# Router logits on four column tiles, fewer count products, scatters without order between them, and a few background steps at other places

## The chip, the cores and the metric

One Trainium2 chip, and the kernel runs on one of its cores. The metric is the device time of one execution in microseconds (us), of which the median over runs counts. TensorE is called PE (its weight loads PEld), VectorE DVE, ScalarE ACT, GpSimd POOL, and SyncE, which issues most DMA transfers, SP.

## The reference

Three layers follow one another. B = 2, S = 768, H = 8 heads of 64, D = 512.

1. Attention: each query row sees the first 8 columns and the last 96 before it, with a linear bias by distance (a slope for each head), softmax, and a product with v.
2. A mixture of 8 experts (512 to 1024 to 512). Each row has eight logits `x @ w_gate` and a local gate `x @ w_local`. The row's own best expert is taken if the local gate is under 0.5, else the expert of the row before it (so the choice is a scan along the sequence). Only the chosen expert is computed, and its output is scaled by the softmax of the logits at that expert.
3. A channel mix: each row is mixed with the row before it, `k = relu(xk @ w_k)`, `out = sigmoid(xr @ w_r) * (k*k @ w_v)`. The last weights come as 64-bit floats and are decoded by integer operations.

All products are to be as good as float32. A float32 product is one matmul in the code and two records of PE in the trace. Expert products are made of three single-pass products, of the upper and lower parts of both operands (`whi`, `wlo` for weights; `xh`, `xl` for rows). A transpose is one record.

## The kernel before

The attention loop (lines 1112 to 1198) has an iteration i for every half of the heads of a tile t of 128 rows: t = i // 2, g = i % 2. The whole program is under a manual schedule: every engine runs its instructions in the order in which the lines emit them. An iteration emits: transposes of the probabilities of i-1 (`emit_pT`, bank PT), the point "Ra", exponentials of i (`emit_exp`, ACT), copies of the transposes out of PSUM (`emit_ev`, the first on DVE, the second on ACT), in odd i the copy of the attention output `emit_xT`, the point "Dm", a step of background work for the first expert (`bg_early`), scores of the next tile (`emit_S`, in odd i), in even i transposes of k and q, in odd i the transposes of a finished tile (`turn_x`), the point "Rb", another `bg_early`, the minima of i+1 (`emit_min`, four DVE passes over the scores, which also add the bias), `route_x` in odd i (DVE scales the turned tile to X), the point "Db", in even i the products with v (`emit_pv`), "Rc", "Dc", and at most one scatter. In the trace, iteration 9 begins at 41.53 us, 13 at 58.32, 17 at 74.99, 18 at 80.60, 19 at 86.42, 20 at 91.17, 21 at 96.43, 22 at 103.14, and the part written out after the loop (lines 1200 to 1282) at 107.92.

The router works on groups of two tiles. `plan` hangs its steps on the named points of iterations (`at`, `do`): logits (`route_lg`, line 200: for every tile four products with xT as the weights, 128 columns, and 18 moving columns of `wgb`), their row maxima (`route_max`, `route_max2`), a transpose to rows (`route_rows`), the scan (`route_scan`, DVE), back to columns (`route_turn`), one-hot (`route_oh`), counts (`route_sum`, lines 273 and 275: `tri[:, 0]` sums the rows before in the tile, `tri[:, 1]` all rows of an earlier tile, `acc` is the sum of earlier groups), and positions (`route_pos`, line 291 on). All of them use one PSUM bank, R. The last group runs behind the loop, between steps of the first expert.

After the third and the fourth group `order_a` and `order_b` (lines 311 to 326) rank the experts by the rows so far, and `early_start` reads the number of the likely first and second expert into SP, which then loads its weights. `bg_early` moves the first expert on by a step: it loads a chunk of weights, makes the lower part of one half chunk on DVE (`w_lo1`, line 630) and the upper part of the next one on ACT (`w_hi1`, line 625), which it appends to `lo_q`. `F_(m)` runs m steps of the first expert's products.

`scatter` (line 283) writes the 128 rows of X of a tile to their places in the DRAM tensor `xs` by an indirect DMA that POOL issues. Behind the scatter of tile 7 SP loads the first rows of the first expert (`early_x`, line 948), behind that of tile 9 the next. From 113 us on PE runs the experts, and from about 300 us the channel mix.

Of the kernel before, what the change touches and what calls it, by code (L numbers as in the profile page):

```python
# [8 lines left out]
F32 = mybir.dt.float32  # L9
# [7 lines left out]
P = 128  # L17
# [27 lines left out]
FREE = 4  # L45
NIN = 4
# [7 lines left out]
class Net:  # L54
# [29 lines left out]
    def routing_consts(self):  # L84
# [4 lines left out]
        self.wgb = c.tile([P, KD, 2, E + 1], F32, name="wgb")  # L89
# [47 lines left out]
    def gate_rest(self):  # L137
        for a in range(2):
            r = slice(a * HD, (a + 1) * HD)
            self.nc.gpsimd.tensor_copy(self.wgb[r, :, a, :], self.wg[r, :, :])  # L140
# [53 lines left out]
    def route_lg(self, g, t, xT, tag="R"):  # L194
        nc = self.nc
        if t == g[0]:
            self.lgp = self.bank(tag, 2 if tag == "PT" else 1)
        for kk in range(KD):
            o = ((t - g[0]) * H + 2 * kk) * (E + 1)
            nc.tensor.matmul(self.lgp[:, o:o + 2 * (E + 1)], lhsT=xT[:, kk, :],  # L200
                             rhs=self.wgb[:, kk, :, :].rearrange("p a c -> p (a c)"), start=True, stop=True)

    def route_max(self, pool, g):
        nc, n, t0 = self.nc, len(g), g[0]
        lh = pool.tile([P, n * H, E + 1], F32, tag="lh", bufs=1, name=f"lh{t0}")
        nc.vector.tensor_tensor(lh, self.lgp[:, 0:n * H * (E + 1)].rearrange("p (a c) -> p a c", c=E + 1),
                                self.RI[:, t0:t0 + n, :].rearrange("p a h -> p (a h)").unsqueeze(2).to_broadcast([P, n * H, E + 1]), op=ALU.mult)
# [59 lines left out]
    def route_sum(self, pool, g):  # L267
        nc, n, t0 = self.nc, len(g), g[0]
        pp = self.bank("R", 1)
        for i in range(n):  # L270
            rest = [self.OHr[:, t0 + a, :] for a in range(i)] + ([self.acc] if self.acc is not None else [])
            o = pp[:, i * E:(i + 1) * E]
            nc.tensor.matmul(o, lhsT=self.tri[:, 0, :], rhs=self.OHr[:, t0 + i, :], start=True, stop=not rest)
            for a, x in enumerate(rest):
                nc.tensor.matmul(o, lhsT=self.tri[:, 1, :], rhs=x, start=False, stop=a == len(rest) - 1)
        one = self.tri[:, 1, 0:1].bitcast(F32)
        parts = [self.OHr[:, t, :].bitcast(F32) for t in g] + ([self.acc.bitcast(F32)] if self.acc is not None else [])
        for a, x in enumerate(parts):
# [299 lines left out]
def build(ctx, tc, ins, out):  # L578
# [4 lines left out]
    n.xs = n.dram.tile([E * REG, D], F32, name="xs")  # L583
    ys = n.dram.tile([ROWS, D], F32, name="ys")
# [387 lines left out]
    def lg(g):  # L972
        for t in g:
            n.route_lg(g, t, xTs[t])

# [7 lines left out]
    for g in groups:  # L983
        i = 2 * g[-1] + 3
        lgg, mx, mx2, rows, scan, tn, oh, sm_, ps_, acc = (lambda f=f, g=g: f(ap2, g) for f in (
            lambda _, g: lg(g), n.route_max, n.route_max2, n.route_rows, n.route_scan, n.route_turn, n.route_oh, n.route_sum,
# [4 lines left out]
        at(i, "Rb", lgg)  # L991
        at(i + 1, "Dm", mx, mx2)
# [16 lines left out]
        if g[-1] in (5, 7):  # L1009
            e = g[-1] == 7  # L1010
            at(i + 3, "Db", lambda e=e: n.order_a(ap2, "fg"[e], n.cnte if e else n.cnt6, n.fvec if e else None))
            at(*((i + 4, "Ra") if e else (i + 3, "Dc")), lambda e=e: n.order_b(ap2, "fg"[e], rp))
            at(i + 4, "Rb", lambda e=e: early_start(3 * e, e))

    with tc.manual_schedule():
# [96 lines left out]
        for i in range(NI - 1):  # L1112
# [40 lines left out]
            emit_min(i + 1)  # L1153
# [8 lines left out]
            if scq:  # L1162
                scatter(scq.pop(0))
# [52 lines left out]
        emit_ev(i - 1, 0)  # L1216
        emit_ev(i - 1, 1, True)
# [10 lines left out]
        while hi_q or lo_q:  # L1228
            bg_early()
# [3 lines left out]
        oh()  # L1233
        emit_pT(i, 0)
# [728 lines left out]
```

## Time and profile before

| | |
|---|---|
| device time, median of 3 runs (lowest, highest) | 487.65 us (485.9, 492.04) |
| the profiled execution's own time | 488.38 us |
| its span from the first to the last instruction | 486.3 us |
| PE busy | 469.6 us, 97% of the span |
| DVE, ACT, POOL busy | 344.4, 265.5, 114.4 us |
| mean granted clock of PE | 0.99 of full speed |

Times in the rows are in us from the start of the span. A row of a timeline has its start, its length, the engine, the line, the operation, out<-in and shapes, how many instructions were merged into it, and in brackets how long the engine was idle before it and for whom. The length of a matmul holds the time until its result is there, so lengths overlap, and the distance between two starts is what one costs. A row of a table by stages has the stretch, its length, and for each engine the time that it was busy and its instructions; then PE's granted clock (1.00 is 2.4 GHz, 0.50 is 1.2 GHz), the share of the DMA engines, and GB/s.

### The profile page before, as it was taken

What the parts mean: (1) busy time and instruction counts of PE and PEld (TensorE: products, weight loads), DVE (VectorE), ACT (ScalarE), POOL (GpSimd) and SP (SyncE); (2) the same over time, 40 slices, a digit from 0 to 9 for tenths busy, and PEclk for the clock granted to TensorE, in tenths of its full rate; (3) what the DMA queues carried; (4) which work ended last, traced back from release to release, by engine and by line L of the source; (5) the groups of instructions that cost most, each with busy time, mean ns of one, the idle gap of its engine ahead of it and who ended that gap; (6) DMA issues with size and microseconds to landing.
All of it is one profiled execution on the core that took longest, in us unless ns stands there. A gap on an engine that the chain in (4) does not pass through costs nothing. (4 is left out here: it accounts for less than half of the span.)

```text
span 486.3 us, 9258 instructions
## 1 busy us (share of the span) xinstructions
PE 469.6 (97%) x3211; PEld 407.0 (84%) x3211; DVE 344.4 (71%) x911; ACT 265.5 (55%) x652; POOL 114.4 (24%) x200
## 2 busy tenths in 40 slices
PE   7999999889999999999999999999999999999994
PEld 5788888778788989878978887798989899898984
DVE  7877796696875885897898888797857768264301
ACT  4787876764536554757587776862433414152320
POOL 4111212112110000010010013051754918253220
PEclk9999998989999999999999999999999999999998
DMA  9998585962775978598699753003836442200001
GB/s 181 266 234 165 145 175 153 290 201 83 255 278 167 355 207 325 171 345 288 238 344 378 278 177 97 34 1 90 301 109 246 146 155 82 65 23 23 22 3 49
DMA packets 76492, 86.90 MB, mean 179 GB/s; under 512 B 50677, under 2 KB 50933, under 8 KB 76437
## 3 DMA queue, kind: packets, MB, share of 16 engines
q1 hardware_dynamic: 68176, 63.01, 42.3%
q0 software_dynamic: 4944, 17.17, 10.9%
q10 hardware_dynamic: 3316, 6.03, 3.4%
q8 instruction: 28, 0.46, 0.4%
q14 instruction: 28, 0.22, 0.2%
HBM read 73.49 MB, written 12.71 MB: 177 GB/s over the span
## 5 line engine op out<-in xcount | busy, mean ns | idle before, releaser
L625 ACT ACTIVATE whi<-wraw 128x512 fp32r<-128x512 f32 x128 | 72.5, 623 | 6.1 <-ACTq L717 2.3
L634 DVE TENSOR_TENSOR wlo<-wraw,whi 128x1024 fp32r<-128x1024 f32 x55 | 66.0, 1217 | 2.7 <-ACT whi L625 2.5
L1474 ACT ACTIVATE sq<-S 128x256 f32<-128x256 f32 x48 | 18.5, 385 | 74.4 <-PE S L643 71.3
L641 PE MATMUL S<-xkh,whi 128*128 128x256 f32 x192 | 54.5, 284 | 0.2 <-ACT whi L625 0.2
L643 PE MATMUL S<-xkh,wlo 128*128 128x256 f32 x192 | 53.6, 279 | 0.2 <-DVE wlo L630 0.2
L642 PE MATMUL S<-xkl,whi 128*128 128x256 f32 x192 | 53.5, 279 | 0.0
L1484 POOL TENSOR_TENSOR kl<-sq,kh 128x256 fp32r<-128x256 f32 x40 | 36.5, 921 | 71.1 <-issue 37.4
L1514 DVE TENSOR_TENSOR o<-O,sig 128x512 f32<-128x512 f32 (+1 forms) x13 | 8.4, 649 | 51.9 <-PE O L643 31.7
L642 PE MATMUL O<-wlo,kh 128*128 128x512 f32 (+1 forms) x104 | 39.3, 378 | 0.3 <-DVE wlo L630 0.3
L643 PE MATMUL O<-whi,kl 128*128 128x512 f32 (+1 forms) x104 | 39.3, 378 | 0.0
L641 PE MATMUL O<-whi,kh 128*128 128x512 f32 (+1 forms) x104 | 39.1, 376 | 0.0
L641 PEld LDWEIGHTS S<-xkh,whi 128*128 128x128 f32 x192 | 36.4, 190 | 0.7 <-ACT whi L625 0.4
L643 PEld LDWEIGHTS S<-xkh,wlo 128*128 128x128 f32 x192 | 36.0, 188 | 0.4 <-DVE wlo L630 0.4
L642 PEld LDWEIGHTS S<-xkl,whi 128*128 128x128 f32 x192 | 36.1, 188 | 0.3
L1475 DVE SCALAR_TENSOR_TENSOR sq<-S,sq 128x256 f32<-128x256 f32 x48 | 20.1, 420 | 16.4 <-ACT sq L1474 16.0
L1483 ACT ACTIVATE kh<-sq 128x256 fp32r<-128x256 f32 x48 | 19.7, 412 | 12.0 <-DVE sq L1475 12.0
L892 ACT ACTIVATE zbig<-zbig,nm 128x232 f32<-128x232 f32 (+1 forms) x48 | 22.4, 466 | 5.9 <-DVE nm L880 5.9
L283 POOL DMA_INDIRECT xs<-X,posi x12 | 12.5, 1045 | 53.1 <-DVE acc L301 21.1
L642 PEld LDWEIGHTS O<-wlo,kh 128*128 128x128 f32 x104 | 19.6, 188 | 4.6 <-DVE wlo L630 0.7
L641 PEld LDWEIGHTS O<-whi,kh 128*128 128x128 f32 x104 | 19.6, 188 | 3.8
L643 PEld LDWEIGHTS O<-whi,kl 128*128 128x128 f32 x104 | 19.6, 188 | 3.7
L892 ACT ACTIVATE peb<-peb,nm 128x232 f32<-128x232 f32 (+1 forms) x48 | 22.2, 463 | 0.0
(461 smaller groups left out, 1423.0 us busy)
## 6 DMA issues: line engine op xcount, KB each, us to landing
wraw<-in_moe_w_dram SPq DMA_DIRECT2D x64, 512.0 KB, 5.7
dwt<-in_moe_w_v_dram POOLq DMA_DIRECT2D x8, 512.0 KB, 4.6
z<-in_moe_w_k_dram SPq DMA_DIRECT2D x8, 512.0 KB, 4.2
z<-in_moe_w_v_dram SPq DMA_DIRECT2D x8, 512.0 KB, 4.8
ys<-yo ACTq DMA_DIRECT2D x13, 256.0 KB, 6.5
vn<-in_v_dram SPq DMA_DIRECT2D x12, 256.0 KB, 4.1
xn<-xs SPq DMA_DIRECT2D x12, 256.0 KB, 5.3
dwt<-in_moe_w_k_dram POOLq DMA_DIRECT2D x6, 512.0 KB, 6.8
```

The source lines that it names most:

```text
L283: self.nc.gpsimd.indirect_dma_start(self.xs, bass.IndirectOffsetOnAxis(ap=self.posi[:, t:t + 1], axis=0), X[t], None)
L625: nc.scalar.activation(out=whl[r, c][0][:, sl], in_=raws[r, c][:, sl], func=ACTF.Copy)
L634: nc.vector.tensor_tensor(lo, raws.pop((r, c)), hi.bitcast(F32), op=ALU.subtract)
L641: nc.tensor.matmul(out_, lhsT=ah, rhs=bh, start=first, stop=False)
L642: nc.tensor.matmul(out_, lhsT=ah, rhs=bl, start=False, stop=False)
L643: nc.tensor.matmul(out_, lhsT=al, rhs=bh, start=False, stop=last)
L892: nc.scalar.activation(out=pe, in_=pe, func=ACTF.Exp, scale=-1.0, bias=nm[:, h:h + 1], accum_out=sm[:, h:h + 1])
L1474: nc.scalar.activation(out=sq_, in_=ps[:, 0:TB], func=ACTF.Relu)
L1475: nc.vector.scalar_tensor_tensor(sq_, ps[:, 0:TB], 0.0, sq_, op0=ALU.max, op1=ALU.mult)
L1483: nc.scalar.activation(out=hh, in_=sq_, func=ACTF.Copy)
L1484: (nc.gpsimd if b else nc.vector).tensor_tensor(hl, sq_, hh.bitcast(F32), op=ALU.subtract)
L1514: nc.vector.tensor_tensor(o[:, a:z], ps[:, 0:z - a], sig[b, i][:, a:z], op=ALU.mult)
```

## The change

The logits of the first five groups get another form. `wgb`, now padded to 32 columns for each of the four 128-row chunks, is the weights, and xT moves with 128 columns; the four chunks stand on four column tiles of PE (`route_lgt`, at the place of the old products). ACT copies the result to SBUF (`route_lge`, at "Db"), and one iteration later PE transposes it, once for each tile (`route_lgb`, at "Ra"). The last group keeps the old form with the new padding. `route_sum` makes the positions of a group in three products (two in the first group) in place of five (three). The scatters write through views of `xs` that are declared disjoint, so that none waits for another, and the end of an iteration may issue two of them. `bg_early` leaves the newest entry of `lo_q` for the next call while the loop runs. For the second ranking, `order_a` goes from "Db" of iteration 20 to "Db" of 19, right behind the positions, and `order_b` from "Ra" of 21 to "Ra" of 20. The minima of iteration 23 go from the loop's last iteration to the part behind it, behind a copy out of PSUM.

```diff
-        self.wgb = c.tile([P, KD, 2, E + 1], F32, name="wgb")
+        self.wgb = c.tile([P, KD, GW], F32, name="wgb")
...
+    def route_lgt(self, pool, g, xTs):
+        nc, n = self.nc, len(g)
+        bank = self.bank("R", 1)
+        for i, t in enumerate(g):
+            for kk in range(KD):
+                nc.tensor.matmul(bank[kk * GW:(kk + 1) * GW, i * P:(i + 1) * P], lhsT=self.wgb[:, kk, :], rhs=xTs[t][:, kk, :],
+                                 start=True, stop=True, tile_position=(0, kk * GW))
+        self.lgp = bank
+
+    def route_lge(self, pool, g):
+        n = len(g)
+        self.lgt = pool.tile([P, 2, P], F32, tag="lgt", bufs=1, name=f"lgt{g[0]}")
+        self.nc.scalar.activation(out=self.lgt[:, 0:n, :], in_=self.lgp[:, 0:n * P].rearrange("p (a c) -> p a c", a=n), func=ACTF.Copy)
+
+    def route_lgb(self, pool, g):
+        self.lgp = self.bank("R", 1)
+        for i in range(len(g)):
+            self.nc.tensor.transpose(self.lgp[:, i * P:(i + 1) * P], self.lgt[:, i, :], self.ident)
...
-        for i in range(n):
-            rest = [self.OHr[:, t0 + a, :] for a in range(i)] + ([self.acc] if self.acc is not None else [])
-            o = pp[:, i * E:(i + 1) * E]
-            nc.tensor.matmul(o, lhsT=self.tri[:, 0, :], rhs=self.OHr[:, t0 + i, :], start=True, stop=not rest)
-            for a, x in enumerate(rest):
-                nc.tensor.matmul(o, lhsT=self.tri[:, 1, :], rhs=x, start=False, stop=a == len(rest) - 1)
+        parts = [(0, n, self.tri[:, 0, :], self.OHr[:, t0:t0 + n, :].rearrange("p a e -> p (a e)"))]
+        if self.acc is not None:
+            parts.append((0, n, self.tri[:, 1, :], self.acc.unsqueeze(1).to_broadcast([P, n, E])))
+        if n > 1:
+            parts.append((1, n, self.tri[:, 1, :], self.OHr[:, t0, :]))
+        for i, (a, z, w, x) in enumerate(parts):
+            nc.tensor.matmul(pp[:, a * E:z * E], lhsT=w, rhs=x, start=i == 0, stop=i == len(parts) - 1)
...
-        self.nc.gpsimd.indirect_dma_start(self.xs, bass.IndirectOffsetOnAxis(ap=self.posi[:, t:t + 1], axis=0),
+        self.nc.gpsimd.indirect_dma_start(self.xviews[t], bass.IndirectOffsetOnAxis(ap=self.posi[:, t:t + 1], axis=0),
...
+    n.xviews = dram_disjoint_views(n.xs, NTT)
...
         at(i, "Rb", lgg)
+        at(i, "Db", lambda g=g: n.route_lge(ap2, g))
+        at(i + 1, "Ra", lambda g=g: n.route_lgb(ap2, g))
...
-            at(i + 3, "Db", lambda e=e: n.order_a(ap2, "fg"[e], n.cnte if e else n.cnt6, n.fvec if e else None))
-            at(*((i + 4, "Ra") if e else (i + 3, "Dc")), lambda e=e: n.order_b(ap2, "fg"[e], rp))
+            at(i + 3 - e, "Db", lambda e=e: n.order_a(ap2, "fg"[e], n.cnte if e else n.cnt6, n.fvec if e else None))
+            at(i + 3, "Ra" if e else "Dc", lambda e=e: n.order_b(ap2, "fg"[e], rp))
...
-        def bg_early():
+        def bg_early(keep=1):
             if ld_q:
                 w_load(0, ld_q.pop(0))
-            for u in lo_q[:1]:
+            for u in lo_q[:1] if len(lo_q) > keep else ():
...
-            emit_min(i + 1)
+            if i < NI - 2:
+                emit_min(i + 1)
...
-            if scq:
+            for _ in scq[:2]:
                 scatter(scq.pop(0))
...
         emit_ev(i - 1, 0)
+        emit_min(i)
         emit_ev(i - 1, 1, True)
...
-        while hi_q or lo_q:
-            bg_early()
+        for _ in range(2):
+            bg_early(0)
         emit_pv(i - 1, 0)
         emit_pv(i - 1, 1)
         tn()
         oh()
+        while hi_q or lo_q:
+            bg_early(0)
```

## Rows read from the trace of the kernel before

**Rows 1.** Busy time by stages: one group of the loop, its last iterations, the experts.
```profile
58.32:74.99 16.67, 16.06 (x165) 13.80 (x163) 13.79 (x64) 12.66 (x44) 2.55 (x7) 1.00 0.70 153
91.17:107.92 16.75, 14.17 (x139) 12.07 (x136) 14.86 (x65) 12.10 (x36) 2.54 (x3) 0.90 0.72 219
153.00:300.00 147.00, 145.82 (x853) 126.47 (x852) 121.77 (x205) 97.21 (x197) 11.46 (x20) 1.00 0.77 268
```
**Rows 2.** The same view of the two stretches in which the granted clock fell.
```profile
80.80:84.20 3.40, 3.40 (x18) 3.07 (x18) 2.45 (x15) 1.75 (x6) 0.00 (x0) 0.50 0.99 263
104.50:107.90 3.40, 3.40 (x33) 3.09 (x32) 3.23 (x17) 2.57 (x7) 0.00 (x0) 0.53 0.97 287
```
**Rows 3.** Timeline of PE in iterations 5 and 6: logits, transposes, products with v.
```profile
27.61 1.86 PE L200 MATMUL R<-wgb,xT 128*128 128x18 f32 x16
29.32 0.31 PE L899 MATMUL PT<-ident,zbig 128*128 128x128 f32 x1
...
30.23 0.60 PE L823 MATMUL S<-ident,kn 128*128 128x128 f32 x4
30.66 0.60 PE L823 MATMUL S<-ident,qn 128*128 128x128 f32 x4
31.46 0.39 PE L924 MATMUL O<-pt,vp 128*64 128x128 f32 x4
31.68 0.39 PE L924 MATMUL O<-pt,vn 128*64 128x128 f32 x4
```
**Rows 4.** Timeline of ACT around the logits of iteration 13.
```profile
63.54 0.39 ACT L908 ACTIVATE pt<-PT 128x256 f32<-128x256 f32 x1 [1.95 <-PE PT L899]
```
**Rows 5.** Timeline of PE: first and last of the five count products of a group.
```profile
55.56 0.25 PE L273 MATMUL R<-OH,tri 128*128 128x8 f32 x1
...
56.01 0.25 PE L275 MATMUL R<-acc,tri 128*128 128x8 f32 x1
```
**Rows 6.** Timeline of PE before the first fall of the clock, and during it.
```profile
78.79 1.96 PE L200 MATMUL R<-wgb,xT 128*128 128x18 f32 x16 [0.24 <-DVE fi L339]
...
82.15 1.06 PE L823 MATMUL S<-ident,kn 128*128 128x128 f32 x4
```
**Rows 7.** Timeline of PE: its two longest waits of the loop.
```profile
93.10 0.30 PE L899 MATMUL PT<-ident,zbig 128*128 128x128 f32 x1 [1.28 <-DVE mm L291]
...
98.43 0.20 PE L320 MATMUL R<-dgg,ones 8*8 8x8 f32 x2 [0.91 <-DVE dgg L315]
```
**Rows 8.** Timeline of DVE in iterations 19 to 21.
```profile
90.39 0.69 DVE L630 TENSOR_TENSOR wlo<-wraw,whi 128x512 fp32r<-128x512 f32 x1 [1.96 <-ACT whi L625]
...
92.87 0.16 DVE L291 SCALAR_TENSOR_TENSOR mm<-iota_e,R 128x16 f32<-128x16 f32 x1
...
93.80 0.67 DVE L910 COPY pt<-PT 128x512 f32<-128x512 f32 x1
...
97.98 0.15 DVE L313 SCALAR_TENSOR_TENSOR keyg<-Rf,keyg 8x1 f32<-8x1 f32 x1
98.16 0.22 DVE L315 TENSOR_SCALAR dgg<-ident,keyg 8x8 f32<-8x8 f32 x1
```
**Rows 9.** Timeline of ACT: first split of the first expert, and that of its fifth chunk.
```profile
89.74 0.61 ACT L625 ACTIVATE whi<-wraw 128x512 fp32r<-128x512 f32 x1
...
112.39 1.14 ACT L625 ACTIVATE whi<-wraw 128x512 fp32r<-128x512 f32 x2
```
**Rows 10.** Timeline of POOL: the scatters of tiles 6 and 7.
```profile
93.93 1.00 POOL L283 DMA_INDIRECT xs<-X,posi  x1 [3.69 <-DVE acc L301]
99.46 0.96 POOL L283 DMA_INDIRECT xs<-X,posi  x1 [4.54 <-DMA xs<-X,posi]
```
**Rows 11.** Timeline of SP: the fifth chunk, and the first rows of the first expert.
```profile
90.68 2.10 SPq L596 DMA_DIRECT2D wraw<-in_moe_w_dram  x1
102.28 0.36 SPq L948 DMA_DIRECT2D xe<-xs  x1
```
**Rows 12.** The page's part on DMA issues: size and median us to landing.
```profile
wraw<-in_moe_w_dram SPq DMA_DIRECT2D x64, 512.0 KB, 5.7
```

More of the change, by code (lines that the diff above doesn't have):

```diff
@@ L5 @@
 from concourse import mybir
+from concourse.ap import dram_disjoint_views
 from concourse._compat import with_exitstack
@@ L45 @@
 FREE = 4
+GW = 32
 NIN = 4
@@ L139, in gate_rest @@
             r = slice(a * HD, (a + 1) * HD)
-            self.nc.gpsimd.tensor_copy(self.wgb[r, :, a, :], self.wg[r, :, :])
+            self.nc.gpsimd.tensor_copy(self.wgb[r, :, a * (E + 1):(a + 1) * (E + 1)], self.wg[r, :, :])
     def mix_rest(self):
@@ L198, in route_lg @@
         for kk in range(KD):
-            o = ((t - g[0]) * H + 2 * kk) * (E + 1)
+            o = ((t - g[0]) * KD + kk) * GW
             nc.tensor.matmul(self.lgp[:, o:o + 2 * (E + 1)], lhsT=xT[:, kk, :],
-                             rhs=self.wgb[:, kk, :, :].rearrange("p a c -> p (a c)"), start=True, stop=True)
+                             rhs=self.wgb[:, kk, 0:2 * (E + 1)], start=True, stop=True)
+    def route_lgt(self, pool, g, xTs):
[14 more added lines that the diff above has]
+            self.nc.tensor.transpose(self.lgp[:, i * P:(i + 1) * P], self.lgt[:, i, :], self.ident)
     def route_max(self, pool, g):
@@ L205, in route_max @@
         lh = pool.tile([P, n * H, E + 1], F32, tag="lh", bufs=1, name=f"lh{t0}")
-        nc.vector.tensor_tensor(lh, self.lgp[:, 0:n * H * (E + 1)].rearrange("p (a c) -> p a c", c=E + 1),
-                                self.RI[:, t0:t0 + n, :].rearrange("p a h -> p (a h)").unsqueeze(2).to_broadcast([P, n * H, E + 1]), op=ALU.mult)
+        nc.vector.tensor_tensor(lh.rearrange("p (m a) c -> p m a c", a=2),
+                                self.lgp[:, 0:n * P].rearrange("p (m r) -> p m r", r=GW)[:, :, 0:2 * (E + 1)].rearrange("p m (a c) -> p m a c", a=2),
+                                self.RI[:, t0:t0 + n, :].rearrange("p t (k a) -> p (t k) a", a=2).unsqueeze(3).to_broadcast([P, n * KD, 2, E + 1]), op=ALU.mult)
         lp = self.LS[:, t0:t0 + n, :]
@@ L970, in do @@
             f()
-    def lg(g):
-        for t in g:
-            n.route_lg(g, t, xTs[t])
     def pos(g):
@@ L985, in build @@
         lgg, mx, mx2, rows, scan, tn, oh, sm_, ps_, acc = (lambda f=f, g=g: f(ap2, g) for f in (
-            lambda _, g: lg(g), n.route_max, n.route_max2, n.route_rows, n.route_scan, n.route_turn, n.route_oh, n.route_sum,
+            lambda _, g: n.route_lgt(ap2, g, xTs), n.route_max, n.route_max2, n.route_rows, n.route_scan, n.route_turn, n.route_oh, n.route_sum,
             lambda _, g: pos(g), n.route_acc))
```

## The prediction

> **What bounds the kernel now.** I read the busy time by stages first. In the experts PE is busy for 145.82 of 147 us, and in one group of the router's loop for 16.06 of 16.67 [rows 1]: PE's own work sets the time, and what is saved in the loop should reach the end, since the work behind it is PE's as well. One stretch is different. From 91.17 to 107.92 PE is busy for only 14.17 of 16.75 us and DVE for 14.86: here the two hold each other up. The same view gives the granted clock, which fell to 0.50 and 0.53 in two stretches of 3.4 us, at 80.8 and at 104.5 [rows 2]. Last I read the timelines, since a length of a matmul overlaps the next, and only the distance of starts is a price [rows 3].
>
> **Logits.** Now: two tiles by four products by two records, from 27.61 to 29.32 (the first transpose behind them), 1.71 us, 0.107 a record [rows 3]. After: again 16 records, but on four column tiles, then two transposes. A transpose costs (30.66 - 30.23) / 4 = 0.11 [rows 3], so 0.22. The products with v show two column tiles: four records of 128 moving columns take 31.68 - 31.46 = 0.22, two at a time at 0.11 [rows 3]. Four column tiles are in no row. The low end is four at a time, 16 / 4 x 0.11 = 0.44; the high end one after the other, 16 x 0.11 = 1.76. The nearest row overlaps fully, so I take 0.50, a little over the low end. Passing into the tiled form costs something: the eight transposes from 30.23 are over at 31.09, and the second four of the v products start at 31.46, so the first four had 0.37 in place of 0.22, 0.15 more. Passing back I take as 0.10 (nothing and 0.15 are its ends). Sum 0.22 + 0.50 + 0.25 = 0.97, and 0.74 saved in a group. Four of the five groups lie before iteration 19, where PE sets the time: 2.95 us. The fifth, in iteration 21, lies in the stretch that DVE holds up, and I count it as nothing (0.74 is its end).
>
> **The copy and the waits of this path.** The ACT copy is 128x256, 0.39 us as the copy of that size at 63.54, ahead of which ACT had been idle for 1.95 us [rows 4]; that idle time hides it. ACT waits for PE there, and what queues behind it are exponentials whose minima come later anyway. Without cover it would be 0.39 in each of five groups, 2 us. PE's transposes of the copy stand behind the eight transposes of the probabilities, 8 x 0.11 = 0.9 us of work, against 0.39 and the two hand-overs. Where a batch begins there are only four of those, and a wait of up to 0.4 is the end. The shared bank R is free at both places but one: the logits still wait for the rank's read, as the 0.24 at 78.79 [rows 6]. The larger memset and the regrouped read of DVE move the same 144 columns: nothing.
>
> **Counts.** Five products of 0.11 (55.56 to 56.01 is four) [rows 5] become three: 0.22 saved, 0.11 in the first group. Six groups give 1.21. Those of the fourth and fifth group fall where DVE sets the time; the rest is 0.11 + 3 x 0.22 = 0.77. The doubled width, 16 columns, costs nothing that a row would show.
>
> **The clock.** A stretch of 3.4 us at half clock costs 3.4 x (1 - 0.50) = 1.7, the second 1.6 [rows 2]. Just before the first fall PE stood still for the rank (0.24 and the result's way before it) and then ran the logits, which move 18 columns a record for 1.8 us [rows 6]; the second follows logits of the same kind behind the second ranking's read. The group from 58.32, whose logits have no such wait, ran at 1.00 [rows 1]. After the change the long run of tiny moves becomes a short one of full width, and I expect the first fall to go: 1.7 us. The second lies over DVE's stretch: nothing (1.6 is its end). The Trainium skill (TensorE: Matmul & The Clock Gate, Part 4: PE-mode transpose) says that transposes do not count as busy for the clock, and this speaks against the change, which takes real products out of a run of transposes; by it both falls stay. The trace bears it out in part only: the half clock ended at 84.2 though nearly all that ran in it were transposes, such as the four of 1.06 us at 82.15 [rows 2, 6]. That result is a rival below.
>
> **The lower parts, the keys, the minima.** Now DVE waits 1.96 us at 90.39 for the upper part that ACT begins only at 89.74 [rows 8, 9], and the minima of iteration 20 and X stand behind it; PE then waits 1.28 at 93.10, and 0.91 at 98.43 for the ranking's key [rows 7]. With the newest entry left in the queue the lower part follows an upper part that is a call old, so the 1.96 goes. Late next is the ranking: `order_b` now stands on PE ahead of the transposes of k and q, and waits for the counts' whole chain, 93.80 - 92.87 = 0.93 from first step to the sum of groups and 0.40 for the key (97.98 to 98.38) [rows 8]. Against it PE has the eight transposes of the probabilities, 0.9 us, so PE waits some 0.5 to 0.9 here, in place of the 0.91 later; on DVE the steps of `order_b` stand ahead of the next copy out of PSUM, which waits as long. Then one more lower part, 0.6 us, falls behind the loop, and the minima of 23 (1.3 us) stand between a copy and the scan there; DVE's amount of work is the same. What can be had: at most the 1.96 and DVE's idle 16.75 - 14.86 = 1.89 [rows 1], 3.85; less the new wait, 0.7, and the 0.6 behind the loop, 2.5. I take 2.0. The ends are 0, if the new wait eats it, and 3.85.
>
> **Scatters.** The wait of 4.54 on POOL goes [rows 10]. POOL does nothing else that is urgent, so it is worth nothing by itself; two issues in a row hold POOL for 2.0 us, and the copies of the global columns behind them have as long until their scores are there. But SP's queue is reordered: the read of the first expert's rows, which waits for both scatters, now stands ahead of a v tile, a v window and the fifth weight chunk, which went out at 90.68 while the read went out at 102.28 [rows 11]. With the second scatter issued some 4.5 us earlier the read goes at about 98, the chunk at about 99, and it lands by its median of 5.7 [rows 12] at about 105; ACT first reads it at 112.39, less what the loop gains, about 106 [rows 9]. Covered by an us: nothing; without cover some 3.
>
> **The sum.** 2.95 + 0.77 + 1.7 + 2.0 = 7.4 us. From the profiled execution's own 488.38 that gives 481.0; that execution was 0.73 over the median shown, so against the median 487.65 the sum gives 480.3. 2% is 9.75 us, about what a measurement of this kernel can tell from no change.
>
> **Rivals.**
> - The clock falls as before (the rule above, at work on this kernel's transposes): 480.3 + 1.7 = 482.0; a fall at each of the three other logits too, as products leave them, adds 1.7 each, up to 487. For it: nearly all of the work around the logits is transposes. Against it: the clock's return at 84.2.
> - PE alone sets the time all along, DVE keeping up: 5 x 0.74 + 1.21 + 1.7 + 1.6 + 1.28 + 0.91 = 10.4, so 477.2. Against it: DVE is busy for 89% of the last iterations [rows 1].
> - The column tiles don't overlap: 1.76 for 0.50 in four groups and part of the fifth adds about 5.5: 486. Against it: the v products.
> - Slower: each step from one column tile to the next costs what passing into the tiled form does, 0.15 a record. Then the products take 16 x 0.26 = 4.2 and a group 4.6 in place of 1.71, five groups 14.6 more; with the falls of the clock left, and 0.77 and 2.0 gained, 11.8 slower: 499. It decides from (2.95 + 0.77 + 2.0) / 5, about 1.1 us over my 0.50 for a group's products. Against it: the v products step between two tiles at no price.
>
> **How the numbers follow.** My forecast 0.50, the clock as before 0.20, PE alone 0.16, no overlap 0.08, slower 0.06. The range is 476.5 to 486.0: it takes in the first three but the lowest of the PE case (0.06), and leaves out the slower case, the repeated falls and a part of no overlap (0.12). Faster by over 2%, under 477.9: most of the PE case, 0.12, and the low edge of the forecast, where DVE's gain goes to its end, 0.07: 0.19. Slower by over 2%: 0.05 of the slower case. The rest, 0.76, is within 2%.
>
> **What would show it.** Logits: 16 short records from first to last start in about 0.5 us and a group's loop 0.7 shorter. Counts: three records. Clock: 1.00 throughout the loop. Lower parts: no idle DVE ahead of line 630, and PE's largest wait in iteration 20 at line 320, under 1 us. Scatters: pairs 1 us apart, and the read of the first expert's rows some 4 us earlier. I am wrong if the 16 records take over 1 us, if the clock falls at other places, or if ACT waits for the fifth chunk.

## The result and the profile after

The changed kernel takes 481.62 us (median of six runs, 480.93 to 483.31) against 488.12 us for the kernel before (six runs, 485.9 to 492.04): a ratio of 0.9865, with a 95% interval of 0.9824 to 0.9905. The forecast was 480.3 us in a range of 476.5 to 486.0, and within 2% as the likeliest outcome; it held. In the two profiled executions the span falls from 486.3 to 479.4 us, 6.9 us against the 7.4 of the sum. How that 6.9 is made up is another matter, and most of what follows is about it.

First the page of the kernel after: the engines' busy time and share of the span.

```profile
PE 460.3 (96%) x3210; PEld 395.9 (83%) x3210; DVE 344.9 (72%) x911; ACT 266.4 (56%) x657; POOL 115.1 (24%) x200
```
Busy time by stages, against [rows 1, 2]; the columns are the stretch, its length, then busy time and instructions of PE, PEld, DVE, ACT and POOL, the granted clock, the DMA share and GB/s.

```profile
80.80:84.20 3.40, 3.40 (x46) 2.88 (x44) 2.70 (x19) 2.45 (x10) 0.00 (x0) 1.00 0.86 278
104.50:107.90 3.40, 2.90 (x29) 2.17 (x25) 3.40 (x9) 3.20 (x11) 0.00 (x0) 1.00 0.30 110
87.71:101.70 13.99, 11.62 (x141) 9.51 (x139) 12.01 (x53) 11.69 (x36) 2.55 (x3) 1.00 0.81 239
24.00:106.60 82.60, 76.71 (x856) 64.36 (x853) 66.99 (x300) 66.68 (x217) 13.83 (x29) 1.00 0.72 200
153.00:300.00 147.00, 145.23 (x852) 125.35 (x851) 122.12 (x210) 96.75 (x198) 13.89 (x22) 1.00 0.76 265
```
The clock is at 1.00 (2.4 GHz) in the two stretches where it had fallen to half, and in the whole of 24.00 to 106.60; the experts' stage is as full as before. In the last iterations, 87.71 to 101.70, PE is busy for 11.62 of 13.99 us. Its idle time there is 2.37 us, hardly less than the 2.58 of before: the stretch became shorter by the work in it, and a larger share of it is waiting.

The timeline of PE, in order of time; the columns are start, length, engine, line, operation, tiles and shape, and in brackets the idle time before it and who ended it. Most lines of the loop are 22 to 24 higher in the new kernel; the making of `X` is line 188 (186 before).

```profile
7.61 0.44 PE L863 MATMUL PT<-ident,kn 128*128 128x128 f32 x2
7.89 0.38 PE L863 MATMUL PT<-ident,qn 128*128 128x128 f32 x2
...
27.45 0.64 PE L210 MATMUL R<-xT,wgb 128*32 128x128 f32 x16
28.03 0.33 PE L923 MATMUL PT<-ident,zbig 128*128 128x128 f32 x1
...
28.96 0.38 PE L222 MATMUL R<-ident,lgt 128*128 128x128 f32 x2
...
45.98 0.30 PE L923 MATMUL PT<-ident,zbig 128*128 128x128 f32 x1 [1.01 <-DVE X L188]
...
54.81 0.26 PE L298 MATMUL R<-OH,tri 128*128 128x16 f32 x1
...
55.03 0.25 PE L298 MATMUL R<-OH,tri 128*128 128x8 f32 x1
...
61.66 0.30 PE L923 MATMUL PT<-ident,zbig 128*128 128x128 f32 x1 [0.38 <-DVE X L188]
...
79.21 0.30 PE L923 MATMUL PT<-ident,zbig 128*128 128x128 f32 x1 [0.73 <-DVE X L188]
...
89.61 0.19 PE L343 MATMUL R<-dgg,ones 8*8 8x8 f32 x2 [0.79 <-DVE dgg L338]
...
99.03 0.30 PE L923 MATMUL PT<-ident,zbig 128*128 128x128 f32 x1 [1.34 <-DVE X L188]
...
106.64 0.48 PE L665 MATMUL S<-whi,exexh 128*128 128x512 f32 x1
```
These answer to [rows 3, 5, 6, 7]. The sixteen records of a group's logits now run from 27.45 to 28.03, 0.58 us where they took 1.71; the counts of a group are three records, 0.11 apart. New are the four waits for `X` (line 188): 1.01, 0.38, 0.73 and 1.34, 3.46 us together. Before, PE had one such wait in the loop's later part, of 0.15 us. The bank in which the new transposes of x stand must be read by DVE before PE may fill it again with probabilities, and the long logits used to run in just that time. The first product of the first expert starts at 106.64; in the execution of before it started at 112.73. I use this record as the loop's end below.

The other engines, against [rows 8 to 11]: the scatters on POOL, the reads on SP, the fifth chunk's split on ACT, and one wait on DVE.

```profile
89.03 1.00 POOL L306 DMA_INDIRECT xs<-X,posi  x1 [2.02 <-DVE keyg L334]
90.33 0.97 POOL L306 DMA_INDIRECT xs<-X,posi  x1 [0.31 <-issue]
```
```profile
93.76 0.34 SPq L972 DMA_DIRECT2D xe<-xs  x1
...
94.79 0.43 SPq L620 DMA_DIRECT2D wraw<-in_moe_w_dram  x1
```
```profile
106.08 1.14 ACT L649 ACTIVATE whi<-wraw 128x512 fp32r<-128x512 f32 x2
```
```profile
45.14 0.69 DVE L188 TENSOR_TENSOR X<-PT,RI 128x512 f32<-128x512 f32 x1 [0.97 <-DMA xs<-X,posi]
```
The scatters are 1.3 us apart and none waits for the one before it; the read of the first expert's rows goes out at 93.76 in place of 102.28; the fifth chunk is asked for at 94.79, which is about the 99 of the prediction less what the loop had gained by then (3.8 at the head of iteration 21), and ACT splits it at 106.08 with no wait. On DVE no idle time stands ahead of the lower parts any more, but `X` of iteration 9 waits 0.97 us for a scatter to land, since `X` has three buffers: that is what PE's wait of 1.01 at 45.98 comes from.

### The profile page after: what moved, and what is told of

The parts are those of the page before. It is cut to its first block, busy times and chain, and to the rows that moved or that the text cites. A ratio compares the mean times of both kernels' runs of the same rounds, so it can differ in the third digit from the quotient of the medians.

```text
span 479.4 us, 9267 instructions
## 1 busy us (share of the span) xinstructions
PE 460.3 (96%) x3210; PEld 395.9 (83%) x3210; DVE 344.9 (72%) x911; ACT 266.4 (56%) x657; POOL 115.1 (24%) x200
```

## The experiments

Times are medians; each is compared with runs of the kernel before taken beside it (medians 488.10, 488.01 and 488.11). "First product" is the start of the first expert's first product on PE. Executions differ in when the loop begins, as the first experiment shows, so I also give it reduced to the start of the profiled execution of before: by the difference of its first transposes of the probabilities from 10.36, where they start there. Two executions of variants of the new kernel (a fourth buffer of X, counts as before) start late, at 13.11; they are reduced by what they lag behind after at iteration 4, 2.44 and 2.47. A bracket behind a time holds the lowest and the highest run, the ratio to before, and its 95% interval.

**One more execution of before.** No edit.

> The kernel before, one more profiled execution, to see whether the two falls of the clock (80.8 to 84.2 and 104.5 to 107.9 us at half) belong to the kernel or to the one execution shown. Theory A, on which the predicted sum rests: the falls belong to the kernel, the clock column shows them again at these places, and the first expert's first product starts at 112.7. Rival B: they come in some executions only (14 of the 19 runs of before in the last comparison had a mean clock of 0.996 or more over the span, where two falls of 3.4 us leave at most 0.993); then the column stays at 1.00 from 24 to 110 us, and counted from the start of the loop the first product comes some 2.5 to 3.4 us sooner, at about 109.5 to 110.2 with the start as before. In that case the share of the gain that I put down to the clock (1.7 us) is not there in most runs.

The run took 488.12 us, its span is 486.1. The stretch from iteration 2 to the first product, and then PE's timeline:

```profile
24.00:112.39 88.39, 83.89 (x889) 73.13 (x888) 69.65 (x314) 68.05 (x220) 13.98 (x29) 1.00 0.75 194
```
```profile
8.60 0.69 PE L839 MATMUL PT<-ident,kn 128*128 128x128 f32 x2
...
82.82 0.31 PE L899 MATMUL PT<-ident,zbig 128*128 128x128 f32 x1
...
83.73 0.60 PE L823 MATMUL S<-ident,kn 128*128 128x128 f32 x4
...
93.71 0.30 PE L899 MATMUL PT<-ident,zbig 128*128 128x128 f32 x1 [1.28 <-DVE mm L291]
...
112.39 0.48 PE L641 MATMUL S<-whi,exexh 128*128 128x512 f32 x1
```
Rival B holds: the clock is 1.00 all through, and the four transposes of k behind the logits take 0.60, where in [rows 6] they took 1.06. The two executions part in two places. This one starts late: its first transposes are slow, such as two of kn at 8.60, 0.49 us to the next group at 9.09, where the execution of after has them in 0.28 (7.61 to 7.89 above). From 5.9 to 13.6 us its transposes stand 0.21 us apart and not 0.11, which is the pace that they have in the recorded falls [rows 6]. The clock is given as 1.00 in both executions all the same, so the record does not show what slowed them. At iteration 4 this execution is 2.46 us behind (22.15 against 19.69), from iteration 10 on 2.20. It then runs past both places where the other fell: its lag goes from 2.22 at iteration 18 to 0.60 at iteration 20, so the first fall cost the other 1.62 us, and at the first product the other is behind by 0.34, so the second cost 0.94. (That is a price net of a wait: with no second fall, this execution waits 0.70 us at 110.21 for a copy out of PSUM, which the other does not.) Without the falls the execution of before would have had its first product at 110.2. In the fourteen traces of this document every execution with a fall in or just behind the loop has a mean clock of 0.995 or less over its span, and every one without has 0.996 or more; below I take this as the sign of at least one fall in runs without a trace. Of the 47 further runs of before, 13 have 0.995 or less; their median is 488.68, that of the other 34 is 487.88. So most executions of before have no such falls and are hardly shorter, perhaps because more of them start late; no trace of each shows that. The Trainium skill (TensorE: Matmul & The Clock Gate, Part 1: What's actually happening) says that the number of slow products at a kernel's start differs from run to run. The two traces agree, and here that is worth 2.2 to 2.5 us.

**Old logits in the kernel after.**

```
-            lambda _, g: n.route_lgt(ap2, g, xTs), n.route_max, ...
+            lambda _, g: lg(g), n.route_max, ...
...
-        at(i, "Db", lambda g=g: n.route_lge(ap2, g))
-        at(i + 1, "Ra", lambda g=g: n.route_lgb(ap2, g))
```


> The changed kernel with the old logits (18 moving columns, no copy, no transposes back); all else changed. Theory A (the forecast's terms add up): the logits are worth 2.95 us and the clock 1.7, so 481.6 + 4.65 = 486.3. Theory B (the short logits laid DVE's work on X bare): PE's waits for X, 3.5 us in iterations 10, 14, 18 and 22, vanish again while the logits cost 5 x 0.92 = 4.6 more, so +1.1 us, and with the clock's falls back (1.7 to 3.3) 484.4 to 486.0; the waits of PE for X go under 1 us in all. By both, at least one fall of the clock comes back.

484.35 us (483.42 to 485.47, 0.9926 of before, 0.9901 to 0.9951). PE's waits for `X` in the loop's later part are gone (the one of 0.45 at iteration 4 is in before, too), and the clock falls twice again. The time is 2 us under that of theory A and at the lower end of theory B.

```profile
80.40:83.60 3.20, 3.20 (x20) 2.87 (x20) 2.99 (x17) 2.31 (x7) 0.00 (x0) 0.51 0.85 266
100.90:104.10 3.20, 3.20 (x24) 2.80 (x24) 2.58 (x12) 1.52 (x6) 0.00 (x0) 0.51 0.99 319
```
All eight runs of this kernel have a mean clock of 0.990 to 0.994; all twelve runs of after have 0.996 or more. So with the long logits a fall comes in every run here, and in the kernel before in about one of four, and with the new logits in none of after. Why the same logits bring it in every run of one kernel and in few of the other is not shown. The rest of the change is worth 3.7 us by itself, falls and all.

**New logits alone in the kernel before.**

```
-            lambda _, g: lg(g), n.route_max, ...
+            lambda _, g: n.route_lgt(ap2, g, xTs), n.route_max, ...
...
+        at(i, "Db", lambda g=g: n.route_lge(ap2, g))
+        at(i + 1, "Ra", lambda g=g: n.route_lgb(ap2, g))
```


> The kernel before with nothing changed but the logits. Theory A: 488.1 - 2.95 - 1.7 = 483.5. Theory B: 488.1 - 1.1 - 1.7 = 485.3, with waits of PE for X as long as in the changed kernel or longer. By both the clock stays at 1.00 through the loop.

481.98 us (481.27 to 484.62, 0.9888, 0.985 to 0.9925), nearly the whole effect, and less than either theory gave (483.5 and 485.3). PE's timeline:

```profile
78.04 0.30 PE L922 MATMUL PT<-ident,zbig 128*128 128x128 f32 x1 [0.74 <-DVE X L188]
...
88.70 0.30 PE L922 MATMUL PT<-ident,zbig 128*128 128x128 f32 x1 [1.28 <-DVE mm L313]
...
94.03 0.20 PE L342 MATMUL R<-dgg,ones 8*8 8x8 f32 x2 [0.90 <-DVE dgg L337]
...
99.52 0.30 PE L922 MATMUL PT<-ident,zbig 128*128 128x128 f32 x1 [1.37 <-DVE X L188]
...
107.51 0.47 PE L664 MATMUL S<-whi,exexh 128*128 128x512 f32 x1
```
The first product is at 107.51, 2.7 us ahead of the 110.2 of a before without falls. The old waits of 1.28 and 0.90 [rows 7] still stand, and two of the waits for `X` stand beside them. The parts don't add: 6.1 for the logits and 3.7 for the rest, 6.5 together. As I read it, both shorten stretches of PE that lie against the same chain on DVE, and each by itself leaves that chain a part of the other's time; no run tests this.

**Lower parts at once again.**

```
-            for u in lo_q[:1] if len(lo_q) > keep else ():
+            for u in lo_q[:1]:
```


> The kernel after, with the first expert's lower parts taken at once again (keep 0). Theory A (the lower parts made DVE idle behind ACT's split, and what stood behind them on DVE was late): DVE is idle 1.3 to 2.0 us ahead of the lower part in iteration 19, the minima of iteration 20 are late by that, and TensorE waits for them; 482.4 to 483.6. Rival B (the idle time is covered by the next wait on the same chain, that for the keys): 481.3 to 482.2, the first product within 0.4 us of 106.6.

484.77 us (483.55 to 488.4, 0.9941, 0.9916 to 0.9965): more than theory A gave. PE's timeline and the busy time behind it:

```profile
91.20 0.30 PE L923 MATMUL PT<-ident,zbig 128*128 128x128 f32 x1 [1.50 <-DVE mm L314]
...
92.62 0.19 PE L343 MATMUL R<-dgg,ones 8*8 8x8 f32 x2 [0.79 <-DVE dgg L338]
```
```profile
93.20:96.80 3.60, 3.60 (x32) 3.27 (x32) 3.53 (x14) 3.04 (x9) 0.96 (x1) 0.53 0.38 146
```
The wait of before is back at the head of iteration 20, 1.50 us, and now with that for the keys 1.4 us behind it; right after them PE's clock falls to half (1.2 GHz) for 3.4 us. From iteration 20 to 22 this kernel takes 12.62 us where after takes 9.32: 3.3 more, 1.5 of them the wait, and most of the rest the clock. Eleven of its twelve runs have a mean clock of 0.995 or less, as this one. (Up to iteration 6 this execution had also lost 2 us to waits that begin with a late q tile; they have no part in that difference.)

**Keys at their old place.**

```
-            at(i + 3 - e, "Db", lambda e=e: n.order_a(...))
-            at(i + 3, "Ra" if e else "Dc", lambda e=e: n.order_b(...))
+            at(i + 3, "Db", lambda e=e: n.order_a(...))
+            at(*((i + 4, "Ra") if e else (i + 3, "Dc")), lambda e=e: n.order_b(...))
```


> The kernel after, with the second set of keys at its old place (built an iteration later, product at the head of iteration 21). Theory A (the key chain's place decides): TensorE's wait of 0.79 us at the head of iteration 20 goes, and one of about 0.9 us for the keys comes at the head of iteration 21, and the early rows' reads are issued one iteration on; the first product at 106.6 to 107.2, 481.6 to 482.4. Rival B (the keys ahead of the sums held the sums' releases too): the first product within 0.3 us earlier, 481.0 to 481.6.

481.79 us (479.92 to 485.78, 0.9891, 0.9853 to 0.993), which can't be told from after. The trace can:

```profile
92.42 0.20 PE L343 MATMUL R<-dgg,ones 8*8 8x8 f32 x2 [0.27 <-DVE dgg L338]
...
105.51 0.47 PE L665 MATMUL S<-whi,exexh 128*128 128x512 f32 x1
```
At its old place the key product waits 0.27 us, not 0.9: with the rest of the change in, the keys are early there. The first product is at 105.7 reduced, 0.9 ahead of after. Of this, 0.32 comes at iteration 10, where this execution waits 0.68 for `X` and not 1.01, which the edit has no part in; 0.66 comes between the heads of iterations 20 and 22. Rival B was nearer, and undersized: by the trace the keys' move loses 0.66 us in this kernel.

**A fourth buffer of X.**

```
-        self.ones = c.tile([8, 256], F32, name="ones")
+        self.ones = c.tile([8, P], F32, name="ones")
...
-        X[t] = pool.tile([P, D], F32, tag="X", bufs=3, ...)
+        X[t] = pool.tile([P, D], F32, tag="X", bufs=4, ...)
...
-        br = pool.tile([1, 2 * P], F32, tag="br", bufs=1, ...)
+        br = pool.tile([P, 2 * P], F32, tag="lgt", bufs=1, ...)[0:1, :]
```


> The changed kernel with four buffers for X in place of three (the row of the scan and the copied logits share a tile, the tile of ones is half as wide, to make room). Theory B: DVE's wait of 0.97 us at 45.14 for the scatter that reads the oldest X goes, and PE's wait of 1.01 behind it: 481.6 - 1.0 = 480.6. Rival: DVE's own order is what holds X up there too: no change, 481.6.

481.79 us (480.5 to 482.99, 0.9868, 0.9835 to 0.9901): no difference from after that the runs show. In the trace the wait at the head of iteration 10 is gone, and the first product, at 107.69 in an execution that starts late like the second one of before, reduces to 105.2, 1.4 ahead of after: 1.06 at iteration 10, and the rest at iteration 14, where it has no wait for `X` either. One trace does not show that the buffer did it: "Counts as before" below starts as late, has three buffers, and no wait at iteration 10. The executions with four buffers that start near after do ("Three moves" and "Two moves"): they have no wait at iteration 10, and the one at iteration 14 is back (0.45 and 0.44). So it is the wait at iteration 10 that the buffer takes away, 1.01 and 0.60 in the two traces of after.

**X ahead of the minima.**

```
+            if g == 1 and i > 1:
+                n.route_x(ap, X, t - 1)
             if i < NI - 2:
                 emit_min(i + 1)
-            if g == 1 and i > 1:
-                n.route_x(ap, X, t - 1)
```


> The changed kernel with X made ahead of the four minima in odd iterations (DVE's order alone). Theory B: PE's waits for X in iterations 14, 16, 18 and 22 (0.38, 0.44, 0.73, 1.34) go, since X is ready 1.3 us sooner: 1.5 to 2.9 us less, 479 to 480. Rival: the minima come 0.6 us later, the exponentials behind them and the transposes behind those too, in each of 11 pairs of iterations: no gain, or up to 3 us slower, 481.6 to 485.

489.25 us (486.57 to 492.13, 1.0026 of before, 0.9997 to 1.0055): 7.6 over after, and no theory had that. DVE, then PE:

```profile
47.42 0.69 DVE L188 TENSOR_TENSOR X<-PT,RI 128x512 f32<-128x512 f32 x1 [4.24 <-DMA xs<-X,posi]
```
```profile
48.26 0.30 PE L923 MATMUL PT<-ident,zbig 128*128 128x128 f32 x1 [2.05 <-DVE X L188]
...
94.50 0.19 PE L343 MATMUL R<-dgg,ones 8*8 8x8 f32 x2 [2.06 <-DVE dgg L338]
```
`X` now waits 4.24 us for the landing of a scatter, which holds its buffer, and behind it on DVE stand the minima, behind those the exponentials and PE's transposes. In after the minima stand ahead, so the landing has that much longer. The first product comes at 112.7 reduced, 6.1 later. PE's waits from 24 us to the first product sum to 8.4 us against 5.9 in after, and the clock is at half from 94.9 to 98.3, just behind the wait of 2.06, which costs about 1.7: 4.2 of the 6.1 are found, the rest I have not placed. All twelve runs have a mean clock of 0.995 or less.

**Three moves, each against a wait of after.** The fourth buffer as above, and

```
-            at(i + 3, "Ra" if e else "Dc", lambda e=e: n.order_b(...))
+            at(i + 3, "Rb" if e else "Dc", lambda e=e: n.order_b(...))
...
+            if g:
+                bg_early()
             do(i, "Rb")
-            bg_early()
+            if not g:
+                bg_early()
```


> The kernel after with three moves, each aimed at one wait that the trace of after shows on TensorE: a fourth buffer of X (the wait of 1.01 us at 45.98), the key product of iteration 20 behind that iteration's score products instead of at its head (0.79 us at 89.61), and in odd iterations the first expert's lower part ahead of the pick's cast, in 1.0 us in which DVE is idle at 95.2, instead of behind it (0.6 of the 1.34 us at 99.03). Theory A (these waits are on the path that sets the end): first product 106.6 - 2.4 = 104.3 with the start as in after, span 477.0, median 479.0 to 479.8. Rival B (what is won ahead of the first expert is given back, since the next wait on the same chain grows): 480.8 to 482.0.

481.18 us (479.54 to 482.47, 0.9862, 0.9827 to 0.9897). PE's timeline, SP's, and the busy time at the loop's end:

```profile
104.49 0.44 PE L948 MATMUL O<-pt,vp 128*64 128x128 f32 x4 [1.82 <-DMA vp<-in_v_dram]
```
```profile
95.44 0.41 SPq L838 DMA_DIRECT2D vp<-in_v_dram  x1
96.06 2.98 SPq L620 DMA_DIRECT2D wraw<-in_moe_w_dram  x3
```
```profile
105.60:109.40 3.80, 3.80 (x22) 3.46 (x22) 1.32 (x6) 0.60 (x1) 0.00 (x0) 0.55 0.14 53
```
At iteration 22 the kernel is 1.9 us ahead of after (95.65, started 0.5 later, against 97.03). Then PE waits 1.82 us for a v window: the lower part, taken earlier, sends three weight loads out right behind that window's own load (96.06 and 95.44; in after they go out at 97.20). The window takes 9.0 us from its issue to the end of PE's wait; in the execution with the old scatters and minima it lands 6.1 us behind its issue at 100.20. That the three loads slowed it is read from this order, not tested. Behind this wait the clock falls. Rival B holds, with this transfer as the place.

**Two moves: four buffers of X and the keys' old place.** Both edits stand above.

> The kernel after with a fourth buffer of X and the second set of keys at its old place. Theory A (both sit on the path that sets the end and add up): TensorE's wait at the head of iteration 10 is gone (1.4 us up to there by the earlier run with four buffers) and the keys give the 0.9 us that they gave alone; counted from the start of the loop the first expert's first product comes 2.0 to 2.4 us sooner than in after, and the median is 1.5 to 2.3 us below that of after in this comparison. Rival B (what is won is given back at the tail, as the three moves gave 1.8 us back to the load of vp): no wait for vp over 0.3 us if B is wrong, a wait of 1 to 2 us for it if B is right, and then 0 to 0.8 us below after.

**The kernel after once more,** in the same comparison. No edit.

> The kernel after once more, as the yardstick for the others of this comparison. If the clock's falls come with waits of TensorE that this kernel no longer has, its clock stays at 1.00 from 24 to 110 us again and the first product stands 85.9 us behind the wait of iteration 4 as in the first trace; median 481.0 to 482.2. If the falls come by chance, one of them may show, and the first product is 1 to 2.6 us later.

Two moves: 481.57 us (480.13 to 483.33, 0.9883, 0.9854 to 0.9912). After: 481.94 us (481.41 to 484.98, 0.9897, 0.9863 to 0.9931). First products, of the two moves and of after:

```profile
105.43 0.47 PE L665 MATMUL S<-whi,exexh 128*128 128x512 f32 x1
```
```profile
45.95 0.30 PE L923 MATMUL PT<-ident,zbig 128*128 128x128 f32 x1 [0.60 <-DVE X L188]
...
73.35 0.19 PE L343 MATMUL R<-dgf,ones 8*8 8x8 f32 x2 [0.18 <-DVE dgf L338]
...
106.68 0.47 PE L665 MATMUL S<-whi,exexh 128*128 128x512 f32 x1
```
Reduced they are at 105.1 and 106.3, so the two moves win 1.2 us up to there, not 2.0 to 2.4: after itself waited only 0.60 for `X` in this execution. No wait for the v window comes. In the medians 0.4 us is not a difference; three of the six runs of the two moves have a mean clock of 0.993 or 0.994, so what the moves win may go to a fall of the clock in them, which no trace shows. The clock of after stays at 1.00 throughout the loop a second time, and the first product stands 85.6 us behind the wait of iteration 4, near the 85.9 of the first trace.

**Counts as before.**

```
-        parts = [(0, n, tri0, OHr[t0:t0+n]), (0, n, tri1, acc), (1, n, tri1, OHr[t0])]
-        ...
+        for i in range(n):
+            rest = [self.OHr[:, t0 + a, :] for a in range(i)] + ([self.acc] ...)
+            ...
```


> The kernel after with the counts as before, one tile at a time (seven products for the fourth group instead of three). Theory A (products in order on TensorE cost what their records take, 0.77 us over the four groups as in the prediction): the first product 0.5 to 0.8 us later, 0.4 to 0.8 us over after. Rival B (TensorE waits behind them for DVE anyway): within 0.3 us at the first product, and no difference in the median.

482.3 us (480.89 to 484.54, 0.9891, 0.9854 to 0.9927). PE's timeline:

```profile
108.55 0.47 PE L664 MATMUL S<-whi,exexh 128*128 128x512 f32 x1
```
The counts are five records again from 56.35 on. The first product, in an execution that starts late, reduces to 106.1, 0.2 ahead of the second trace of after; but this execution has no wait for `X` at iteration 10, and that is worth 0.63. Followed from iteration to iteration against that trace, it falls behind by 0.11 at the first group's counts, by 0.21 at the second's, by nothing at the third's and by 0.08 at the fourth's. At the third the wait of 0.18 for the first ranking's key (73.35 above) is gone, and at the fourth that for the second's is 0.67 in place of 0.79. So of the 0.77 that the records of four groups would cost (0.11 + 3 x 0.22) 0.40 reach the first product, and waits behind the counts take up the rest: between the two theories.

**Scatters and last minima as before.**

```
-        self.nc.gpsimd.indirect_dma_start(self.xviews[t], ...
+        self.nc.gpsimd.indirect_dma_start(self.xs, ...
...
-            if i < NI - 2:
-                emit_min(i + 1)
+            emit_min(i + 1)
...
-            for _ in scq[:2]:
+            if scq:
                 scatter(scq.pop(0))
...
-        emit_min(i)
```


> The kernel after with the scatters as before (one tensor for all, one scatter at the loop's foot) and the last minima at their old places. Theory A (both cost nothing on the path, as in the prediction): the early rows are read 2 to 8 us later, no engine waits over 0.5 us for them, and the median lies within 0.5 us of after. Rival B (the later read makes the fifth chunk's load late, or the minima in their old place hold the rows' sums at the tail): ACT waits 1 to 3 us for the fifth chunk or TensorE for the minima, 1 to 3 us over after.

481.27 us (five runs, 480.07 to 483.96, 0.9874, 0.9837 to 0.9912; a sixth took 489.15), not to be told from after in the runs. In the trace it is later by 1.6 us than the second one of after at the first product (107.9 reduced). DVE, POOL, PE:

```profile
45.89 0.69 DVE L188 TENSOR_TENSOR X<-PT,RI 128x512 f32<-128x512 f32 x1 [1.32 <-DMA xs<-X,posi]
```
```profile
96.31 0.96 POOL L306 DMA_INDIRECT xs<-X,posi  x1 [5.43 <-DMA xs<-X,posi]
```
```profile
105.70 0.44 PE L948 MATMUL O<-pt,vn 128*64 128x128 f32 x4 [0.64 <-DVE pt L934]
106.36 0.44 PE L948 MATMUL O<-pt,vp 128*64 128x128 f32 x4 [0.22 <-DMA vp<-in_v_dram]
...
108.33 0.47 PE L665 MATMUL S<-whi,exexh 128*128 128x512 f32 x1
```
A scatter that waits for the one before it holds its `X` longer; DVE waits 1.32 us for that buffer instead of 0.57, and PE 1.36 instead of 0.60 (1.01 in the first trace of after). At the loop's end PE waits 0.64 for a copy and 0.22 for a v window. The wait for the copy stands in two other executions with the last minima at their old place and a full clock there (0.63 with the new logits alone, 0.70 in the second one of before), and in none of the nine executions with the minima at their new place (the one with X ahead of them left aside): the minima's move takes it away. Both theories are half right: no median moves, but the path does.

## Why the prediction came out right, and where its steps were wrong

- **The bound.** Right: what is saved in the loop reaches the end. From the first product to the end takes 372.8 and 372.9 us in the executions of after and 373.6 and 373.7 in those of before. These 0.8 to 0.9 are a difference of two things. In the first 20 us behind the first product after loses 0.6, since the routing of the last groups, between the first expert's steps, is reached sooner and PE waits for DVE there (0.37 at 107.95 for the one-hot, where before has no wait). Then it gains some 1.5 bit by bit between 225 and 320 us behind the first product, where no line of the change runs; every trace of a changed kernel has this gain, and what it is stays open.
- **Logits, 2.95.** The size per group was near: 0.58 for the products with the passage out of the tiled form, 0.22 for the transposes, 0.80 against my 0.97, so 0.91 saved and not 0.74. The 0.58 is 0.14 over four at a time at 0.11, so the four column tiles overlap fully here and stepping between them costs nothing that shows; the slower rival and the one of no overlap fall with that. The Trainium skill (TensorE: Matmul & The Clock Gate, Part 3: Packing small matmuls, Measured speedup vs the span model) gives a speedup of 2.38 times for three column tiles at 512 columns. Here four tiles at 128 columns take 16 records in 0.58 us, where the old form took 1.71, 2.9 times with the passage in it. Four groups would be 3.6 us. What came is 2.7 by the logits alone. The step that failed is "where PE sets the time": I asked what the copy and the bank of the new path would wait for, and not what the long logits had covered, which is DVE's making of `X` out of the bank that PE fills next: four waits of PE, 3.46 us in the trace of after.
- **Counts, 0.77.** Too high: 0.40 by the trace with the old counts, 0.32 of it in the first three groups and 0.08 in the fourth, which I had counted as nothing. At the third and the fourth the next wait for DVE took what the records save; the sixth group, behind the first product, shows nothing (372.9 us from there to the end with the old counts, as in after).
- **The clock, 1.7 and nothing.** The mechanism is borne out in the main: with the short logits no run of after shows a fall (two by their traces, the other ten by their mean clock), and with the long ones put back all eight do. But the long logits are not enough by themselves, since 34 of 47 runs of before show none, and not the only thing that goes ahead of a fall, as the waits in three variants show. The sizes are 1.62, near the 1.7 predicted, and 0.94, where I had counted nothing. What I missed is that the profiled execution was one of the few of before with the falls at all. The Trainium skill (TensorE: Matmul & The Clock Gate, Part 4: PE-mode transpose) says that transposes do not count as busy in the same way. By that I had a rival in which both falls stay, and the traces do not bear it out: the clock of after is 1.00 from 24 to 106.6 us, with more transposes in it than before, and the second execution of before runs its many transposes at 1.00, too. That rival falls.
- **Lower parts, keys, minima, 2.0.** The sum was about right for the wrong reason. The lower parts are worth 3.3, 1.5 of it the wait that I named and most of the rest a fall of the clock behind it. The keys were to leave a wait of 0.5 to 0.9 in place of 0.91; it is 0.79, but the old place would now wait 0.27 only, and their move loses 0.66 (the same between the traces of two moves and of a fourth buffer alone). The minima, which I had counted as nothing but a delay, take away a wait of 0.64 at the loop's end. "PE's largest wait in iteration 20 at the key product, under 1 us" is what the trace shows.
- **Scatters, nothing.** The order came as predicted, pairs 1.3 us apart and the early read 8.5 us sooner (4.7 of it beside the 3.8 that the loop had gained), with the fifth chunk in time. That POOL has nothing urgent was right, that the scatter is worth nothing was not: it holds a buffer of `X`, and DVE and PE wait for that. By the traces this is worth 0.4 to 0.8 us (PE's wait of 1.36 against 1.01 and 0.60), in the medians none.
- **The sum, 7.4.** Between the two profiled executions 6.9: 2.6 of clock (mine 1.7), 3.5 of work in the loop (mine 5.7), 0.8 behind it (mine 0). Three errors offset each other, and that the sum came out is luck in that measure. Between executions that have no falls and start alike it is about 4.3, an estimate from 3.5 + 0.8; the fastest runs, 484.95 and 480.93, are 4.0 apart. The other 2 us of the medians' 6.5 are not accounted for. Falls of the clock, at most 2.6 in 13 of 47 runs of before, make 0.7 on the average; late starts are in the traces of both kernels, and how often each has them is not known without a trace of each run.

## What to carry to other kernels

Before an operation on the bounding engine is shortened, list what ran on the other engines in its time: here a quarter of what four groups' faster products won (2.7 of 3.6 us were left) came back as waits for a PSUM bank and a buffer that the slow ones had covered. A small saving on an engine that waits for another soon after is cut at that wait: of the counts' 0.77 us 0.40 were left. Two executions of one kernel can differ by more than such a saving, so follow both from iteration to iteration, and see where the difference arises, before it is put down to the edit. And a dip of the clock seen in one trace is a price for that execution: take a second trace, or the mean clocks of the runs, before it goes into a sum for the median.

## What the runs showed of the hardware that was not expected

- Four column tiles of 32 columns, float32 with 128 moving columns, run fully beside each other: 16 records in 0.58 us with the passage out of the tiled form, where two transposes in full form take 0.22.
- The first transposes of the probabilities start between 9.81 and 13.11 us in the fourteen traces, 2.75 us apart in two executions of one kernel. In the later one the transposes up to 13.6 us stand 0.21 us apart, the pace of the recorded falls, and not 0.11; the recorded clock is 1.00 there.
- Seven falls of the clock to 1.2 GHz were seen. Three began within 1.4 us of the end of a wait of PE (of 2.06, of 1.82, and of 0.79 with one of 1.50 just ahead of it); waits of 1.28, 1.34 and 1.36 had none behind them, and neither had one of 2.05 (at 48.26, with X ahead of the minima). The other four came behind the long logits, with no wait over 0.24 us in the microseconds ahead. What they have in common stays open.
